# The last w2 product one accumulator at a time, and the gate product directly behind it

## The chip, the cores and the metric

The kernel runs on one core of a Trainium2 chip. The metric is device time in microseconds (us). Each time is one execution; the median of the runs is what counts.

## The reference

```python
def _attn_ref(q, k, v, tau):                   # batch 4, heads 8, seq 576, head_dim 64
    scores = scale * np.matmul(q, k.transpose(0, 1, 3, 2))
    thresh = np.max(scores, axis=-1, keepdims=True) - tau
    scores = np.where(scores >= thresh, scores, -1000000000.0)
    ...
    return np.matmul(attn, v)                  # softmax over the kept scores

def _moe_ref(x, w_gate, w1, w2):               # x [2304, 512], 8 experts, F = 1024
    cap = N // E                               # 288 tokens for every expert
    order = np.argsort(-(x @ w_gate).flatten())
    ...                                        # greedy: best free token/expert pair first
    for e in range(E):
        h = np.maximum(x[mask] @ w1[e], 0.0)
        out[mask] = h @ w2[e]

def _moe2_ref(x, w_gate, w_val, w_out):        # d_ff = 1536
    gate = 1.0 / (1.0 + np.exp(-(x @ w_gate)))
    return gate * (x @ w_val) @ w_out

def reference(...):
    x = attn_out.transpose(0, 2, 1, 3).reshape(B * S, H * D)
    x = _moe_ref(x=x, **moe_kwargs)
    return _moe2_ref(x=x, **moe2_kwargs)
```

## The kernel before

Attention fills the first 365 us or so, in an order written out in a hand table; the change does not touch it. After it the function `experts` does the rest expert by expert, with x, h and y held transposed (features on the partitions, the 288 tokens of one expert along the free axis).

Each float32 operand of a product is held as two parts, a rounded high half and the remainder, and a product of two such operands is three products: high·high, low·high, high·low. With 128-wide slices each product of the program is therefore a run of 12 matmuls of 128x128 by 128x288. High halves are written by ACT, low halves by DVE: `yh`, `xh`, `hh`, `gh` are ACT's, `yl`, `xl`, `hl`, `gl` are DVE's. The first expert's w1 and w2 products are the exception, they are plain float32.

For expert e:

- `arrive(e)`: POOL gathers the rows of x (`xr`, `xs`); PE turns them with twelve transposes in four triples (`ps<-idf,xr` twice and `ps<-idf,xs` once, L1191), and each triple is evicted by `xh` (ACT) and `xl` (DVE, L1142).
- `stage_m(e)`: eight times a w1 product (`ps<-xh,w`, L1147, in a work buffer of PSUM, evicted with relu by `hh` and `hl`) and a w2 product (`acc<-hh,w` and `acc<-hl,w`, L1157, onto four accumulators). Weights `wr` come on SP's queue (L1219, three buffers) and are split by ACT (`w<-wr`, L1228) and DVE (L1055). The four accumulators are then evicted into y: four `yh` on ACT (L1136) and four `yl` on DVE (L1142).
- `stage_g(e)`: twelve times a gate product G (`ps<-yh,wgh` ..., eight matmuls with `yh`, then four with `yl`), a value product V (`ps<-yh,wvh` ...), the sigmoid `sg` (ACT, L1329), `gt` (DVE, L1333), `gh` (ACT, L1337), `gl` (DVE, L1340), and an out product (`acc<-gh,wo`). The weights of G and V stay in SBUF; those of the out product, `wo`, are loaded on SP (L1311). At the end the four accumulators are evicted into `ot`, turned back by 12 transposes (`rows`, `ps<-idf,ot`, L1378) in three groups of four, evicted (`orow`, L1385) and scattered by POOL (L1389).

The **seam** of an expert, in this text, is the place on PE between its last w2 product and its first value product.

PSUM has four accumulator buffers (`ps_acc`), three work buffers (`ps_work`, shared by the w1, G and V products, the triples and the row transposes), and one for the router. `onto` already writes the last of the eight w2 products accumulator by accumulator, so that the first accumulator is complete after three of the twelve matmuls.

Beside this runs the router, which finds the tokens of the next expert. Its wide rounds search a threshold in 8 steps each: a table `kx<-kc` is stored (L747) and read back as 16 broadcasts `kw<-kx` (L751), both on SP's queue; in each step DVE scans it twice (`big<-kw,tw`, L766), writes `rhw` (L769), and PE adds it up (`rps<-rhw`, L772). There are four wide rounds, 32 steps.

The order of the instructions on each engine is written by a planner, `Plan`, before anything runs. Each job has an engine, a planned duration, jobs it depends on, a priority, and buffers it takes or holds. `step` places, over and over, the job that can start first on its engine by the planner's clock. PE has a main chain, the products in their order (`m_seq` and `g_seq`; `main` gives its next job); its other jobs (triples, row transposes, router steps) go first if they are ready by the time PE comes free, and otherwise fill the time until the main chain's head is ready. The last w2 product is one job in this plan: all four `yh` jobs depend on all of it, and G(0) depends on the first three `yh`.

```python
a = job("PE", 1.59, g1, (ydep if j else yhi[:3]) + [ready[3 * j]], None, acq=[hpg], use=hy[e])
a.order = ydep
```

Of the kernel before, what the change touches and what calls it, by code (L numbers as in the profile page):

```python
# [904 lines left out]
class Job:  # L905


    def __init__(self, eng, dur, fn, deps, prio, acq, use, lag):
        self.eng, self.dur, self.fn, self.deps, self.prio, self.acq, self.use, self.lag = eng, dur, fn, deps, prio, acq, use, lag
        self.end, self.order, self.quick = None, [], False  # L910


class Slots:
# [11 lines left out]
class Plan:  # L925
# [16 lines left out]
    def job(self, eng, dur, fn, deps=(), prio=0.0, acq=(), use=(), lag=0.0):  # L942
        j = Job(eng, dur, fn, [d for d in deps if d is not None], prio, acq, use, lag)
        for h in (*acq, *use):
            h.left += 1
        if prio is not None:
            self.queue(j, prio)
        return j
# [24 lines left out]
        return t  # L973

    def step(self):
        best = None
        for e, todo in self.todo.items():
            cand = todo if e == "PE" else todo[:120]
            can = [(r, j) for j in cand for r in [self.ready(j)] if r is not None]
            if e == "PE":  # L980
                main = [(r, j) for j in self.main() for r in [self.ready(j)] if r is not None]
                late = [(r, j) for r, j in can if (r + j.lag if j.prio != -1 else max(r + j.lag, self.spaced)) <= self.free[e]]
                can = late + main + [x for x in can if x not in late]
            free, crit = self.free[e], self.crit
            if crit is not None and crit.eng == e and crit.end is None:
                c = self.ready(crit)
                if c is not None:
                    can = [(r, j) for r, j in can if j is crit or max(r, free) + j.dur <= c]
            if not can:
                continue  # L990
            t = max(free, min(r for r, _ in can))
            if best is None or t < best[0]:
                best = t, next(j for r, j in can if r <= t)
        if best is None:
            return False
        t, j = best
        if j in self.todo[j.eng]:
            self.todo[j.eng].remove(j)
        self.place(t, j)
        return True  # L1000
# [26 lines left out]
def experts(tc, rt, xd, idf, w12, w3in, w3, pre, out):  # L1027
    nc = tc.nc
    V, A, G, SP = nc.vector, nc.scalar, nc.gpsimd, nc.sync
    with (  # L1030
# [14 lines left out]
        job = p.job  # L1045
        big, wdcap, pw, acc = Slots(9), Slots(WD), Slots(3), Slots(1)
# [12 lines left out]
        ready, stored, first_out, first_hold = {}, {}, {}, {}  # L1059
        for n in range(36):  # L1060
            j, kind = divmod(n, 3)
# [85 lines left out]
                nc.tensor.matmul(ps, w(q), x[:, q], start=n == 0, stop=n == 11)  # L1147
                n += 1

        def onto(acc, wh, wl, xh, xl, first, last):  # L1150

            parts = [(i, m) for i in range(3) for m in range(4)]
            if last:
                parts.sort(key=lambda q: q[::-1])
            for i, m in parts:
                w, x = ((wh, xh), (wl, xh), (wh, xl))[i]
                nc.tensor.matmul(acc[m][:, :CAP], w[:, 128 * m : 128 * m + 128], x, start=first and i == 0, stop=last and i == 2)  # L1157
# [47 lines left out]
        def stage_m(e):  # L1205

            seq1, seq2 = [], []
            x_dep = xl_jobs[e]
            hacc = Hold(acc)
            accs = {}  # L1210
            ws = []
            for j in range(8):
                base = pos_m[e] + 2 * j
                hr, h0, h1, hps, hh = Hold(s_wr), Hold(s_w0), Hold(s_w1), Hold(pw), Hold(s_h)
                box = {}

                def load(e=e, j=j, box=box):
                    box["r"] = wp.tile([128, 2, 512], F32, name="wr", bufs=3)
                    SP.dma_start(box["r"], w12[bass.ds(reg[e], 1), j].rearrange("a p (h f) -> (a p) h f", h=2))  # L1219
                    return 524288  # L1220

                ld = job("SP", 0.4, load, [expert_job[e]], base - 10, acq=[hr])
                half = [ld, ld]
                for i, (nm, hd) in enumerate((("w0", h0), ("w1", h1))):

                    def hi(i=i, nm=nm, box=box):
                        box[nm] = wp.tile([128, 2, 512], F32R, name=nm)
                        A.activation(box[nm][:, 0], box["r"][:, i], AF.Copy)  # L1228

                    def lo(i=i, nm=nm, box=box):  # L1230
                        minus(box[nm][:, 1], box["r"][:, i], box[nm][:, 0])

                    pr = base + 2.5 * i - 3
                    if e:
                        a = job("ACT", 0.56, hi, [ld], pr, acq=[hd], use=[hr])
                        half[i] = job("DVE", 0.64, lo, [a], pr, use=[hd, hr])

                def m1(e=e, box=box):
                    box["ps"] = ps_w.tile([128, 512], F32, name="ps")
                    if e == 0:  # L1240
                        for q in range(4):
                            nc.tensor.matmul(
                                box["ps"][:, :CAP], box["r"][:, 0, 128 * q : 128 * q + 128], X[0][0][:, q], start=q == 0, stop=q == 3
                            )
                        return
                    w = box["w0"]
                    thrice(
                        box["ps"][:, :CAP], lambda q: w[:, 0, 128 * q : 128 * q + 128], lambda q: w[:, 1, 128 * q : 128 * q + 128],
                        *X[e],
                    )  # L1250

                def evh(box=box):
                    dt = F32R if e else F32
                    box["h"] = hp.tile([128, CAP], dt, name="hh", bufs=3), hp.tile([128, CAP], dt, name="hl", bufs=3)
                    two(*box["h"], box["ps"][:, :CAP], relu=True)

                def evl(box=box):
                    two_l(*box["h"], box["ps"][:, :CAP], relu=True)

                def m2(j=j, box=box):  # L1260
                    if j == 0:
                        accs["a"] = [ps_a.tile([128, 512], F32, name="acc") for m in range(4)]
                    if e == 0:
                        for m in range(4):
                            nc.tensor.matmul(
                                accs["a"][m][:, :CAP], box["r"][:, 1, 128 * m : 128 * m + 128], box["h"][0], start=j == 0, stop=j == 7
                            )
                        return
                    onto(accs["a"], box["w1"][:, 0], box["w1"][:, 1], *box["h"], j == 0, j == 7)

                own = [h0] if e else [hr]
                a = job("PE", 1.59 if e else 2.12, m1, [half[0]] + x_dep, None, acq=[hps], use=own + hx[e])
                b = job("ACT", 0.32, evh, [a], base - NEAR, acq=[hh], use=[hps])
                if e:
                    b = job("DVE", 0.39, evl, [b], base - NEAR, use=[hps, hh])
                own = [h1] if e else [hr]
                c = job("PE", 1.59 if e else 2.12, m2, [b, half[1]], None, acq=[hacc] if j == 0 else [], use=own + [hh] + ([hacc] if j else []))
                seq1.append(a)
                seq2.append(c)
            ydep, yhi = [], []  # L1280
            for m in range(4):

                def evh(m=m):
                    if m == 0:
                        Y[e] = [bt(h, [128, 4, CAP], f"y{x}", F32R) for h, x in zip(hy[e], "hl")]
                    two(Y[e][0][:, m], Y[e][1][:, m], accs["a"][m][:, :CAP])

                def evl(m=m):
                    two_l(Y[e][0][:, m], Y[e][1][:, m], accs["a"][m][:, :CAP])

                pr = pos_m[e] + 16 - NEAR
                a = job("ACT", 0.32, evh, [c], pr, acq=hy[e] if m == 0 else [], use=[hacc] + (hy[e] if m else []))
                a.order = yhi[:1]
                yhi.append(a)
                ydep.append(job("DVE", 0.39, evl, [a], pr, use=[hacc] + hy[e]))
            m_seq[e] = seq1[:2] + [x for j in range(2, 8) for x in (seq2[j - 2], seq1[j])] + seq2[6:]
            stage_g(e, ydep, yhi)

        def stage_g(e, ydep, yhi):
# [4 lines left out]
            for j in range(12):  # L1304
# [40 lines left out]
                    w = box["wo"] if e else first_out[j]  # L1345
                    onto(accs["a"], w[:, 0], w[:, 1], *box["h"], j == 0, j == 11)

                a = job("PE", 1.59, g1, (ydep if j else yhi[:3]) + [ready[3 * j]], None, acq=[hpg], use=hy[e])
                a.order = ydep
                s = job("ACT", 0.31, sig, [a], base - NEAR, acq=[hsg], use=[hpg])  # L1350
                b = job("PE", 1.59, lambda g1=g1: g1(nm="v"), ydep + [ready[3 * j + 1]], None, acq=[hpv], use=hy[e])
                g1s.append([a, b])
# [206 lines left out]
```

## Time and profile before

| | us |
|---|---|
| median of 3 runs | 1126.08 (1125.22 to 1126.72) |
| the profiled execution | 1126.27 |
| span in its trace | 1124.5 |
| PE, PEld busy | 1053.8, 980.8 |
| DVE, ACT, POOL busy | 788.4, 524.1, 322.5 |

PE is TensorE's matmuls, PEld its weight loads, DVE VectorE, ACT ScalarE, POOL GpSimd, and SPq the DMA queue that SP feeds. All times below are of one profiled execution, in us from the start of the span, which ends 1.8 us short of that execution's own time. The mean granted TensorE clock is 0.983 of full speed.

### The profile page before, as it was taken

Reading aid. Unit: us, or ns where it says so; the run is one execution under the profiler, and the core shown is the slowest. Engines: PE = TensorE matmul, PEld = TensorE weight load, DVE = VectorE, ACT = ScalarE, POOL = GpSimd, SP = SyncE. Lnnn points to the kernel's source line nnn. Section 1 sums busy time; section 2 is a strip of 40 time slices with the busy share of each in tenths; the row PEclk is TensorE's granted clock in tenths of the full one; section 3 lists DMA queues with packets and bytes.
Section 4 is the critical chain, followed back from the end, with each engine's and each line's share of the span. In section 5 each row is a group of like instructions: output and inputs, shape, how many; then the busy total and the mean of one; then the engine's idle time right before and its main releaser. Section 6 shows DMA issues by size and latency. Waiting matters only on the chain.

```text
span 1124.5 us, 21000 instructions
## 1 busy us (share of the span) xinstructions
PE 1053.8 (94%) x7885; PEld 980.8 (87%) x7885; DVE 788.4 (70%) x1915; ACT 524.1 (47%) x1176; POOL 322.5 (29%) x334
## 2 busy tenths in 40 slices
PE   3999999999994899998998999999999999999997
PEld 3788888888883579998997999999999899999996
DVE  7899999999988999876876867866864313412311
ACT  4788898889882233343133125214313413412411
POOL 5888988898840100020010011010101100100101
PEclk9999999999996899999999999999999999999999
DMA  7422424334015676546356347346444433433232
GB/s 265 166 87 98 145 87 137 107 133 139 1 39 201 215 276 241 183 155 161 110 145 186 94 121 211 113 119 179 146 117 152 134 112 119 162 107 123 76 108 84
DMA packets 52885, 156.17 MB, mean 139 GB/s; under 512 B 11568, under 2 KB 16560, under 8 KB 50864
## 3 DMA queue, kind: packets, MB, share of 16 engines
q1 hardware_dynamic: 49712, 145.40, 40.6%
q0 software_dynamic: 3072, 9.44, 2.8%
q8 instruction: 62, 1.02, 0.4%
q14 instruction: 39, 0.32, 0.1%
HBM read 135.38 MB, written 19.43 MB: 138 GB/s over the span
## 4 chain that ended last, share of the span: by engine, by line
PE 53%; issue 26%; DVE 13%; DMA 4%; POOL 2%; ACT 1%; SPq 1%; DVEq 0%; POOLq 0%; ACTq 0%
PE ps L1147 19%; PE acc L1157 11%; PE s L250 7%; PE t L291 4%; PE o L367 2%; PE o L391 2%; DVE nm L261 2%; PE o L375 2%; PE o L363 2%; DVE p L283 1%; DMA wr<-in_w 1%; POOL out L1389 1%; DMA qkr<-in_qk 1%; DVE lo L348 1%; DVE wf L1091 1%
## 5 line engine op out<-in xcount | busy, mean ns | idle before, releaser
L1333 DVE TENSOR_TENSOR gt<-ps,sg 128x288 f32<-128x288 f32 x96 | 43.8, 457 | 146.1 <-PE ps L1147 132.2
L1389 POOL DMA_INDIRECT out<-orow,idx x24 | 22.9, 952 | 423.3 <-ACT orow L1385 397.2
L1329 ACT ACTIVATE sg<-ps 128x288 f32<-128x288 f32 x96 | 39.5, 412 | 199.0 <-PE ps L1147 173.3
L1157 PE MATMUL acc<-gh,wo 128*128 128x288 f32 x768 | 123.0, 298 | 0.0
L265 ACT ACTIVATE e<-s,nm 128x576 f32<-128x576 f32 x144 | 106.3, 738 | 24.8 <-DVE nm L261 23.4
L1055 DVE TENSOR_TENSOR w<-wr,w 128x512 fp32r<-128x512 f32 x112 | 75.4, 689 | 60.1 <-ACT w L1228 59.6
L1147 PE MATMUL ps<-yh,wgh 128*128 128x288 f32 x384 | 107.2, 301 | 9.6 <-DVE xl L1142 7.2
L1337 ACT ACTIVATE gh<-gt 128x288 fp32r<-128x288 f32 x96 | 42.7, 445 | 155.7 <-DVE gt L1333 154.0
L283 DVE SCALAR_TENSOR_TENSOR p<-s,th,e 128x576 f32<-128x576 f32 x128 | 100.7, 810 | 16.2 <-ACT th L269 14.0
L1157 PEld LDWEIGHTS acc<-gh,wo 128*128 128x128 f32 x768 | 108.0, 188 | 1.7 <-issue 1.4
L261 DVE TENSOR_REDUCE nm<-s 128x1 f32<-128x576 f32 x144 | 104.2, 748 | 6.5 <-PE s L250 5.5
L1147 PE MATMUL ps<-yh,wvh 128*128 128x288 f32 x384 | 106.2, 299 | 0.0
L1147 PE MATMUL ps<-yh,wgl 128*128 128x288 f32 x384 | 105.6, 297 | 0.0
L1228 ACT ACTIVATE w<-wr 128x512 fp32r<-128x512 f32 x112 | 69.0, 629 | 77.9 <-PE acc L1157 32.5
L1147 PE MATMUL ps<-yh,wvl 128*128 128x288 f32 x384 | 104.9, 296 | 0.0
L1172 POOL DMA_INDIRECT xr<-xd,idx x16 | 15.2, 950 | 308.1 <-issue 208.8
L250 PE MATMUL s<-kh,qs 128*128 128x288 f32 x320 | 80.1, 333 | 24.2 <-DVE p L283 15.8
L250 PEld LDWEIGHTS s<-kh,qs 128*128 128x128 f32 x320 | 52.9, 197 | 41.9 <-issue 22.8
L1147 PEld LDWEIGHTS ps<-yh,wgh 128*128 128x128 f32 x384 | 72.7, 189 | 10.9 <-DVE xl L1142 5.7
L766 DVE TENSOR_SCALAR_CACHE_REDUCE big<-kw,tw 128x1152 bf16<-128x1152 f32 x56 | 79.0, 1410 | 1.2
L291 PE MATMUL t<-idf,p 128*128 128x128 f32 x548 | 78.2, 276 | 0.7 <-ACT lo L346 0.7
L291 PEld LDWEIGHTS t<-idf,p 128*128 128x128 f32 x548 | 64.5, 142 | 11.7 <-ACT tf L321 2.6
(233 smaller groups left out, 2766.3 us busy)
## 6 DMA issues: line engine op xcount, KB each, us to landing
wo<-wod SPq DMA_DIRECT2D x84, 512.0 KB, 3.6
wr<-in_w SPq DMA_DIRECT2D x64, 512.0 KB, 3.8
qkr<-in_qk SPq DMA_DIRECT2D x15, 1248.0 KB, 5.4
wd<-in_w SPq DMA_DIRECT2D x36, 512.0 KB, 4.4
wod<-wo SPq DMA_DIRECT2D x12, 512.0 KB, 3.4
vr<-in_v SPq DMA_DIRECT2D x16, 320.0 KB, 3.8
kw<-kx SPq DMA_DIRECT2D x64, 72.0 KB, 4.4
xd<-xl SPq DMA_DIRECT2D x8, 512.0 KB, 6.5
```

Source lines behind the costliest of these rows:

```text
L250: nc.tensor.matmul(s[:, h, 0:288], qs[:, qo : qo + 128], kt[:, ko + 288 * h : ko + 288 * h + 288], start=m == 0, stop=m == len(src) - 1,)
L261: nc.vector.tensor_reduce(d[u]["nm", i], d[u]["s", i][:, :, 0:288], op=OP.max, axis=AX.XY, negate=True)
L265: nc.scalar.activation(e, d[u]["s", i][:, :, 0:288], AF.Exp, bias=d[u]["nm", i])
L283: nc.vector.scalar_tensor_tensor(dst.rearrange("p (c n) -> p c n", c=2), w["s", i][:, :, 0:288], nmth[n // 2][1][:, n % 2 : n % 2 + 1], w[ ...
L291: nc.tensor.matmul(t[:m, 128 * j : 128 * j + 128], src, idf, is_transpose=True, start=j == 0, stop=j == len(srcs) - 1, skip_group_check=True,)
L766: v.tensor_scalar(self.big, self.kw[h], thr, None, op0=OP.is_ge, op1=OP.add, accum_out=cnt[:, h : h + 1])
L1055: V.tensor_sub(l, x, h.bitcast(F32))
L1147: nc.tensor.matmul(ps, w(q), x[:, q], start=n == 0, stop=n == 11)
L1157: nc.tensor.matmul(acc[m][:, :CAP], w[:, 128 * m : 128 * m + 128], x, start=first and i == 0, stop=last and i == 2)
L1228: A.activation(box[nm][:, 0], box["r"][:, i], AF.Copy)
L1333: V.tensor_tensor(box["gt"], box["v"][:, :CAP], box["sg"], op=OP.mult)
L1337: A.activation(box["h"][0], box["gt"], AF.Copy)
```

## The change

The last w2 product (j = 7) becomes four jobs of the plan, one for each accumulator, three matmuls each; `yh` of accumulator m depends on the m-th of them alone. G(0) depends on the first `yh` only. And PE is reserved: G(0) carries a mark, `seam`, that names the first `yh`. As soon as that `yh` has its place in the plan and G(0) is the next job of the main chain but not ready, `step` passes PE over as long as any other engine has something to place, so that nothing is put on PE between the w2 product and G(0).

```diff
     def step(self):
+        return self.choose(True) or self.choose(False)
+
+    def choose(self, keep):
...
             if e == "PE":
-                main = [(r, j) for j in self.main() for r in [self.ready(j)] if r is not None]
+                heads = self.main()
+                main = [(r, j) for j in heads for r in [self.ready(j)] if r is not None]
+                if keep and heads and heads[0].seam and heads[0].seam.end is not None and not (main and main[0][1] is heads[0]):
+                    continue
...
-                c = job("PE", 1.59 if e else 2.12, m2, [b, half[1]], None, acq=[hacc] if j == 0 else [], use=own + [hh] + ([hacc] if j else []))
-                seq1.append(a)
+                own = own + [hh] + ([hacc] if j else [])
+                dur = 1.59 if e else 2.12
+                if j < 7:
+                    c = [job("PE", dur, m2, [b, half[1]], None, acq=[hacc] if j == 0 else [], use=own)]
+                else:
+                    c = [job("PE", dur / 4, lambda m=m, m2=m2: m2(ms=[m]), [b, half[1]], None, use=own) for m in range(4)]
+                seq1.append([a])
                 seq2.append(c)
...
-                a = job("ACT", 0.32, evh, [c], pr, acq=hy[e] if m == 0 else [], use=[hacc] + (hy[e] if m else []))
+                a = job("ACT", 0.32, evh, [c[m]], pr, acq=hy[e] if m == 0 else [], use=[hacc] + (hy[e] if m else []))
...
-                a = job("PE", 1.59, g1, (ydep if j else yhi[:3]) + [ready[3 * j]], None, acq=[hpg], use=hy[e])
-                a.order = ydep
+                a = job("PE", 1.59, g1, (ydep if j else yhi[:1]) + [ready[3 * j]], None, acq=[hpg], use=hy[e])
+                a.order, a.seam = ydep, yhi[0]
```

The instructions are the same and as many; each engine runs them in another order from the first seam on (the lines move by 7 to 13). Three places show it.

PE at the second expert's seam, from the end of its last w2 product; `w_7235` is that product's weight tile, L1191 (after: L1198) are the transposes of the next expert's rows. Before:

```order
L1157 MATMUL acc<-hh,w_7235 128x288 x2
L1157 MATMUL acc<-hl,w_7235 128x288
L1191 MATMUL ps<-idf,xr 128x96 x2
L1191 MATMUL ps<-idf,xs 128x96
L1191 MATMUL ps<-idf,xr 128x96 x2
L1191 MATMUL ps<-idf,xs 128x96
L1191 MATMUL ps<-idf,xr 128x96 x2
L1191 MATMUL ps<-idf,xs 128x96
L1147 MATMUL ps<-yh,wgh 128x288
L1147 MATMUL ps<-yh,wgl 128x288
```

After:

```order
L1164 MATMUL acc<-hh,w_7235 128x288 x2
L1164 MATMUL acc<-hl,w_7235 128x288
L1154 MATMUL ps<-yh,wgh 128x288
L1154 MATMUL ps<-yh,wgl 128x288
L1154 MATMUL ps<-yh,wgh 128x288
L1154 MATMUL ps<-yh,wgl 128x288
L1154 MATMUL ps<-yh,wgh 128x288
L1154 MATMUL ps<-yh,wgl 128x288
L1154 MATMUL ps<-yh,wgh 128x288
L1154 MATMUL ps<-yh,wgl 128x288
L1154 MATMUL ps<-yl,wgh 128x288 x4
L1198 MATMUL ps<-idf,xr 128x96 x2
```

The gate product now follows the w2 product at once. One triple went ahead of the w2 product, two follow the gate product.

ACT at the same place. Before:

```order
L1228 ACTIVATE w_7274<-wr 128x512
L1136 ACTIVATE xh<-ps 128x288
L1228 ACTIVATE w_7290<-wr 128x512
L1228 ACTIVATE w_7303<-wr 128x512
L1136 ACTIVATE yh<-acc 128x288 x4
L1136 ACTIVATE xh<-ps 128x288 x3
L1329 ACTIVATE sg<-ps 128x288
```

After:

```order
L1235 ACTIVATE w_7274<-wr 128x512
L1143 ACTIVATE xh<-ps 128x288
L1143 ACTIVATE yh<-acc 128x288 x3
L1235 ACTIVATE w_7302<-wr 128x512
L1143 ACTIVATE yh<-acc 128x288
L1235 ACTIVATE w_7309<-wr 128x512
L1342 ACTIVATE sg<-ps 128x288
L1143 ACTIVATE xh<-ps 128x288 x2
```

Two weight conversions stood ahead of the four `yh`; now three `yh` stand ahead of both, and one of the conversions is between the third and the fourth.

SP's queue in the third expert's w1 and w2 products: `wr` are their weights, `kx` and `kw` the router's table. Before:

```order
L1311 DMA wo<-wod_5001 128x1024
L747 DMA kx<-kc 128x8x18
L1219 ISA
L1219 DMA wr<-in_w 128x1024
L751 DMA kw<-kx 16x1152
L1219 ISA
L1219 DMA wr<-in_w 128x1024
L751 DMA kw<-kx 16x1152 x7
L1219 ISA
L1219 DMA wr<-in_w 128x1024
```

After:

```order
L1324 DMA wo<-wod_5001 128x1024
L1226 ISA
L1226 DMA wr<-in_w 128x1024
L747 DMA kx<-kc 128x8x18
L1226 ISA
L1226 DMA wr<-in_w 128x1024
L751 DMA kw<-kx 16x1152 x4
L1226 ISA
L1226 DMA wr<-in_w 128x1024
L751 DMA kw<-kx 16x1152 x6
```

One weight load moved ahead of `kx`, and the table's reads fall into other groups between the loads.

## Rows read from the trace of the kernel before

**Rows 1.** Page, part 1: busy time, share of the span, instructions.

```profile
PE 1053.8 (94%) x7885; PEld 980.8 (87%) x7885; DVE 788.4 (70%) x1915; ACT 524.1 (47%) x1176; POOL 322.5 (29%) x334
```

**Rows 2.** Page, part 5: busy, mean ns | idle before, releaser.

```profile
L1147 PE MATMUL ps<-yh,wgh 128*128 128x288 f32 x384 | 107.2, 301 | 9.6 <-DVE xl L1142 7.2
```

**Rows 3.** Stretches, PE alone: bounds, length, busy (count), clock, DMA share, GB/s.

```profile
419.32:422.98 3.66, 3.15 (x14) 1.00 0.69 243
514.42:519.56 5.14, 2.61 (x23) 1.00 0.96 245
610.44:615.85 5.41, 2.61 (x24) 1.00 0.63 218
702.21:706.31 4.10, 3.17 (x18) 1.00 0.38 113
790.70:795.24 4.54, 3.02 (x26) 1.00 0.54 174
880.10:888.32 8.22, 5.79 (x39) 0.83 0.65 199
970.00:974.74 4.74, 3.64 (x30) 1.00 0.70 232
1055.84:1058.82 2.98, 2.98 (x26) 1.00 0.00 0
598.32:610.44 12.12, 9.71 (x67) 1.00 0.66 186
```

**Rows 4.** Timeline, second expert's seam: start, length, engine, line, instruction, count [idle before].

```profile
515.16 1.29 ACT L1136 ACTIVATE yh<-acc 128x288 fp32r<-128x288 f32 x4
515.89 1.55 DVE L1142 TENSOR_TENSOR yl<-acc,yh 128x288 fp32r<-128x288 f32 x4
517.35 1.18 DVE L1142 TENSOR_TENSOR xl<-ps,xh 128x288 fp32r<-128x288 f32 x3
517.86 0.40 PE L1147 MATMUL ps<-yh,wgh 128*128 128x288 f32 x1 [2.53 <-DVE xl L1142]
```

**Rows 5.** Timeline, last expert's seam.

```profile
1054.82 1.64 ACT L1136 ACTIVATE yh<-acc 128x288 fp32r<-128x288 f32 x4 [1.58 <-PE acc L1157]
1055.26 1.68 DVE L1142 TENSOR_TENSOR yl<-acc,yh 128x288 fp32r<-128x288 f32 x4 [1.53 <-ACT yh L1136]
1055.84 1.47 PE L1378 MATMUL ps<-idf,ot 128*96 128x128 f32 x12
1057.13 0.40 PE L1147 MATMUL ps<-yh,wgh 128*128 128x288 f32 x1
1058.82 0.30 PE L1147 MATMUL ps<-yh,wvh 128*128 128x288 f32 x1
```

**Rows 6.** Timeline, PE: a triple within an out product; the sixth expert's G.

```profile
673.86 0.33 PE L1191 MATMUL ps<-idf,xr 96*128 96x96 f32 x2
674.05 0.52 PE L1157 MATMUL acc<-gh,wo 128*128 128x288 f32 x2
...
885.42 0.46 PE L1147 MATMUL ps<-yh,wgh 128*128 128x288 f32 x1 [1.87 <-DVE xl L1142]
```

**Rows 7.** Timeline, third expert's w1 and w2 products: SP's queue, ACT.

```profile
585.63 0.37 SPq L747 DMA_DIRECT2D kx<-kc  x1
591.31 0.35 SPq L1219 DMA_DIRECT2D wr<-in_w  x1
597.31 1.15 ACT L1228 ACTIVATE w<-wr 128x512 fp32r<-128x512 f32 x2 [3.15 <-DMA wr<-in_w]
```

**Rows 8.** Timeline, a wide round of the router: PE's wait, DVE's scan and slack.

```profile
530.57 0.17 PE L772 MATMUL rps<-rhw,one 128*128 128x8 bf16 x1 [1.31 <-DVE rhw L769]
545.58 0.46 DVE L1333 TENSOR_TENSOR gt<-ps,sg 128x288 f32<-128x288 f32 x1 [0.48 <-PE rps L772]
546.53 1.41 DVE L766 TENSOR_SCALAR_CACHE_REDUCE big<-kw,tw 128x1152 bf16<-128x1152 f32 x1
550.47 0.46 DVE L1333 TENSOR_TENSOR gt<-ps,sg 128x288 f32<-128x288 f32 x1 [0.49 <-PE rps L772]
```

More of the change, by code (lines that the diff above doesn't have):

```diff
@@ L909, in __init__ @@
         self.eng, self.dur, self.fn, self.deps, self.prio, self.acq, self.use, self.lag = eng, dur, fn, deps, prio, acq, use, lag
-        self.end, self.order, self.quick = None, [], False
+        self.end, self.order, self.quick, self.seam = None, [], False, None
 class Slots:
@@ L1148, in thrice, with onto @@
                 n += 1
-        def onto(acc, wh, wl, xh, xl, first, last):
-            parts = [(i, m) for i in range(3) for m in range(4)]
+        def onto(acc, wh, wl, xh, xl, first, last, ms=range(4)):
+            parts = [(i, m) for i in range(3) for m in ms]
             if last:
@@ L1258, in evl, with m2 @@
                     two_l(*box["h"], box["ps"][:, :CAP], relu=True)
-                def m2(j=j, box=box):
+                def m2(j=j, box=box, ms=range(4)):
                     if j == 0:
@@ L1263, in m2 @@
                     if e == 0:
-                        for m in range(4):
+                        for m in ms:
                             nc.tensor.matmul(
@@ L1268, in m2 @@
                         return
-                    onto(accs["a"], box["w1"][:, 0], box["w1"][:, 1], *box["h"], j == 0, j == 7)
+                    onto(accs["a"], box["w1"][:, 0], box["w1"][:, 1], *box["h"], j == 0, j == 7, ms)
                 own = [h0] if e else [hr]
@@ L1295, in stage_m @@
                 ydep.append(job("DVE", 0.39, evl, [a], pr, use=[hacc] + hy[e]))
-            m_seq[e] = seq1[:2] + [x for j in range(2, 8) for x in (seq2[j - 2], seq1[j])] + seq2[6:]
+            seq = seq1[:2] + [x for j in range(2, 8) for x in (seq2[j - 2], seq1[j])] + seq2[6:]
+            m_seq[e] = [x for y in seq for x in y]
             stage_g(e, ydep, yhi)
```

## The prediction

> **What bounds the kernel now.** I read the busy shares first: PE is at 94% of the span and its weight loads at 87%, against 70% for DVE, 47% for ACT and 29% for POOL [rows 1]. So time can only be won where PE stands still or runs slowly. Next come the groups by line: of the products of the expert stages, the one with real idle time ahead of it is the gate product, 9.6 us, of which 7.2 us ended with DVE's `xl`, an eviction of transposed rows of the next expert [rows 2]. These waits lie at the seams, and the eight seams as stretches (the first eight of rows 3: from the end of the last w2 product to the first value matmul) are 3.66, 5.14, 5.41, 4.10, 4.54, 8.22, 4.74 and 2.98 us [rows 3].
>
> What such a stretch needs is read at the last expert, where the row transposes cover everything: twelve of them start at 1055.84, G starts at 1057.13 and V at 1058.82 [rows 5]. The transposes thus need 1057.13 − 1055.84 = 1.29 and G 1058.82 − 1057.13 = 1.69. Four row transposes are a third, 0.43. A triple of the arriving rows starts at 673.86 and the next product at 674.05, 0.19 [rows 6]; I take 0.25, since that product's first pair is long.
>
> Why the others take more shows best at the second expert [rows 4]. Three triples fill all three work buffers of PSUM. ACT has two weight conversions ahead of the `yh` in its order and begins the first `yh` at 515.16, 0.74 after the w2 product (514.42, the stretch's start). DVE follows with four `yl` until 517.44 and only then does the `xl` that frees a buffer; G starts at 517.86 after 2.53 idle. It is a queueing loss, not a lack of engine time.
>
> **Part 1, the seams: what is lost before.** Stretch minus need (G, plus what is turned inside it):
> - experts 0 to 2: 3.66 − 1.69 − 0.25 = 1.7 (a small product of the router stands there, taken like a triple); 5.14 − 1.69 − 0.75 = 2.7; 5.41 − 1.69 − 0.75 = 3.0;
> - experts 3 and 4: 4.10 − 1.69 − 0.25 = 2.2; 4.54 − 1.69 − 0.86 − 0.25 = 1.7;
> - expert 5: 8.22 − 1.69 − 1.29 − 1.0 = 4.2 (12 row transposes and all four triples). Here the granted clock is 0.83 against 1.00 at the other seams [rows 3]: G starts at 885.42 after 1.87 idle [rows 6] and takes 888.32 − 885.42 = 2.90, so 1.2 of the loss is G partly at the lower level of the clock, 1.2 GHz, behind an idle PE;
> - experts 6 and 7: 4.74 − 1.69 − 1.29 − 0.25 = 1.5; 2.98 − 1.29 − 1.69 = 0.
>
> Sum 17.0 us. The transposes themselves are moved, not removed, and cost the same wherever they stand.
>
> **Part 2, the seams: what is left after.** With G directly behind the w2 product, G(0) waits for `yh` and `yl` alone. The last expert bounds this from below: its first `yh` began at 1054.82, 1.02 before the product's end, the four `yh` ended at 1056.46 and the four `yl` at 1056.94 [rows 5]. A G at 1055.84 would reach its fourth `yh` pair after six matmuls (0.13 each, 1.69/12 rounded down) at 1056.63 and its fourth `yl` matmul at about 1057.3, both later than needed: no wait. The bound from above is that every `yh` still begins 0.74 after the product, as at the second expert. Then the four `yl` end 517.44 − 514.42 = 3.02 behind the product, the last matmul of G follows, and the stretch is about 3.3 instead of 1.69: 1.6 lost at each seam. Where each lies between is set by ACT's and DVE's new order:
> - expert 0: two conversions (1.15 / 2 = 0.6 each [rows 7]) still precede `yh`: 0.7. Expert 1: one conversion between the third and fourth `yh`, and V waits a little for the sigmoid's buffer: 0.7;
> - expert 2: all work buffers are taken by triples ahead of the product, G's is freed by an `xl` behind three `yl`: 1.2. Expert 3: a conversion and an `xh` ahead of the first `yh`, a conversion within: 1.2;
> - expert 4: a router scan of 1.41 [rows 8] stands ahead of `yl` on DVE, partly under the product: 0.9. Experts 5 to 7: 0.4, 0.1, 0.1, with `yh` first in line; at expert 5 PE no longer stands idle, so the clock should hold at 1.00.
>
> Sum 5.3, between 0 and 8 × 1.6 = 13. Seams: 17.0 − 5.3 = **11.7 gained**, between 4 and 17.
>
> **Part 3, what the new order moves elsewhere.**
> - *SP's queue at expert 2.* `kx` is issued at 585.63, and the weight load behind its first read only at 591.31; ACT later waits 3.15 for `wr` [rows 7]. PE's stretch 598.32 to 610.44 is 12.12 with 9.71 busy [rows 3]. It holds five products of 1.6 and some small work of 0.4, so 12.12 − 8.4 = 3.7 are lost. After, one weight load stands ahead of `kx` and the next right behind it. Bounds: 0 and 3.7; I take 2.4, because two of the three late loads move forward.
> - *The router.* At the second expert PE waits 1.31 for `rhw` [rows 8]; how much of that wait stays when everything around it moves is not in the rows; I take 0.8 gained, between a wait twice as long (−1.3) and none (1.3), nearer to none, since in SP's order three more of the table's reads now stand ahead of the weight load of that round, and the wait is for scans of that table.
> - *New costs.* At the last expert three triples now stand directly ahead of the first w1 product, which needs their `xh` and `xl`: the eviction of one, about 0.65 (half of the 1.29 for four `yh`). At the sixth, triples within a value/out pair, 0.25. At the third, a second `rhw` wait, 0.4. Together 1.3 lost, between 0 and 3.
>
> Sum of part 3: 2.4 + 0.8 − 1.3 = **1.9 gained**, between −4 and 5.
>
> **The sum.** 11.7 + 1.9 = 13.6 against the profiled execution's 1126.27: 1112.7. That execution lies 0.2 above the median of the runs, 1126.08, so on the median's footing 1112.5.
>
> **The rivals.**
>
> *Exposed eviction at every seam.* The transposes were the work that covered the eviction of the accumulators; with nothing between, a G that needs `yh` and `yl` waits for them. By the upper bound of part 2 this leaves 1.1 to 1.6 a seam, say 9 to 10 of the 17, and gives about 1126 − 8 = 1118. Against it stands the last expert, where eviction begins under the product itself [rows 5]; for it the second, where it did not [rows 4]. The Trainium skill, page Perfetto Trace Analysis, section Optimizing Tensor Performance, says under Matmuls that independent matmul groups should rotate through PSUM banks so that the evacuation of one overlaps the next group's matmuls; that speaks against this change, which takes the independent group out. The last expert's rows agree only in part: their eviction overlaps the same product's later matmuls as well.
>
> *Absorbed downstream.* PE arrives sooner at waits that other engines pace: `rhw` [rows 8], weight loads [rows 7]. If half of what experts 1 to 4 gain at their seams (9.6 − 4.0 = 5.6) and all of the 1.9 goes there: 1112.5 + 2.8 + 1.9 = 1117; with expert 2's starvation made worse by 2, 1119. For it: these waits exist. Against: after them PE runs back to back, so a gain at a later seam cannot be taken away by an earlier wait.
>
> *Slower.* In a wide round's steps DVE's order had `gt` ahead of the first of the two scans; now it stands between them, and PE's router product between G and V. A step has DVE waiting 0.48 and 0.49 for `rps`, with a period of 550.47 − 545.58 = 4.89 [rows 8], about one G, V and out product. If the second scan slips by more than that slack, each step lengthens. At 0.6 a step beyond the slack, in 30 of the 32 steps, 18 us are lost: 1112.5 + 18 = 1130.5. It turns slower from 13.6 / 30 = 0.45 a step. Against it: `gt` waits only for V, which PE now ends sooner relative to the scan, and 0.48 of slack stands ready.
>
> *It doesn't do what it says.* The order still shows four row transposes ahead of G at expert 6 and the router's product at expert 2; were PE stalled at all seams by something else named in no row, the time stays near 1126.
>
> **How the numbers follow.** Forecast 0.74, exposed eviction 0.11, absorbed 0.09, slower 0.04, no change 0.02 for the last. The predicted time is the forecast's, 1112.5. Its own spread is the unknown residue at the seams (5.3, from 0 upward) and part 3: down by 5.5 to 1107, if nearly no residue stays; up to the two rivals' 1118 and 1119, so the range ends at 1120. What lies outside is the slower case, no change, and tails of the forecast. A measurement here tells about 0.2% (2.3 us) from no change; faster by more than that, below 1123.8, is everything but the last two rivals and a tail: 0.93, same 0.03, slower 0.04.
>
> **What would show it.** In the profile after: the eight stretches between 1.7 and 3.0, with no `xl` as the releaser of `ps<-yh,wgh`; at each seam the first `yh` beginning before the last w2 matmul; the clock at 1.00 at the sixth seam; shorter waits for `wr` around 600; a wide round's step at 4.9 or less. The forecast is wrong if G's waits merely change their name to `yl`, or if the idle time before `rps<-rhw` grows by more than a few us.

## The result, and the profile after

The changed kernel takes 1114.11 us (1113.41 to 1114.60, four runs) against 1126.05 for the kernel before on the same chip: ratio 0.989, 95% interval 0.988 to 0.991. That is 12 us gained, where 13.6 were forecast, and within the range given. The profiled execution took 1113.79 us.

Page, part 1 of the changed kernel, beside [rows 1], and the gate product's line, beside [rows 2]:

```profile
PE 1051.8 (95%) x7884; PEld 979.3 (88%) x7885; DVE 787.2 (71%) x1915; ACT 525.1 (47%) x1176; POOL 323.5 (29%) x334
...
L1154 PE MATMUL ps<-yh,wgh 128*128 128x288 f32 x384 | 106.0, 298 | 2.1 <-DVE xl L1149 1.2
```

Busy times hardly move; the idle time ahead of the gate product falls from 9.6 to 2.1 us. The eight seams, from the end of the last w2 product to the first value matmul, answer to the first eight of [rows 3] (bounds, length, PE busy and count, clock, DMA share, GB/s):

```profile
419.01:421.27 2.26, 2.26 (x15) 1.00 0.49 150
512.87:515.52 2.65, 2.51 (x20) 1.00 0.79 252
604.50:607.58 3.08, 1.84 (x15) 1.00 0.03 8
694.56:697.76 3.20, 2.56 (x17) 1.00 0.13 53
783.64:787.44 3.80, 3.63 (x23) 1.00 0.74 226
873.19:876.29 3.10, 3.09 (x22) 1.00 0.50 168
957.90:960.29 2.39, 2.39 (x23) 1.00 0.59 159
1044.28:1045.88 1.60, 1.60 (x14) 1.00 0.00 0
```

The sum falls from 38.8 to 22.1, and the clock is 1.00 in all of them, also at the sixth, which showed 0.83 before. Not all of the 16.7 is gained, since some transposes now stand elsewhere. The last stretch is G alone: 1.60. With that as the work of G (the prediction took 1.69), 0.11 for a row transpose, 0.25 for a triple and 0.2 for a router product (the prediction took 0.25), what a stretch holds beyond its work is its loss; the eight sum to 17.3 us before and 5.5 after. At the second expert the change looks like this (timeline, beside [rows 4]):

```profile
512.03 1.05 ACT L1143 ACTIVATE yh<-acc 128x288 fp32r<-128x288 f32 x3
512.48 1.18 DVE L1149 TENSOR_TENSOR yl<-acc,yh 128x288 fp32r<-128x288 f32 x3
512.87 0.30 PE L1154 MATMUL ps<-yh,wgh 128*128 128x288 f32 x1
512.98 0.62 ACT L1235 ACTIVATE w<-wr 128x512 fp32r<-128x512 f32 x1
513.50 0.40 ACT L1143 ACTIVATE yh<-acc 128x288 fp32r<-128x288 f32 x1
```

The first `yh` begins 0.84 us before the product ends at 512.87; before, it began 0.74 after it. The conversion between the third and the fourth `yh` still costs G 0.4.

### The profile page after: what moved, and what is told of

Same layout as the page of the kernel before. It is cut to its first block, busy times and chain, and to the rows that moved or that the text cites. A ratio compares the mean times of both kernels' runs of the same rounds, so it can differ in the third digit from the quotient of the medians.

```text
span 1112.0 us, 20994 instructions
## 1 busy us (share of the span) xinstructions
PE 1051.8 (95%) x7884; PEld 979.3 (88%) x7885; DVE 787.2 (71%) x1915; ACT 525.1 (47%) x1176; POOL 323.5 (29%) x334
## 3 DMA queue, kind: packets, MB, share of 16 engines
q8 instruction: 62, 1.02, 0.4%
## 4 chain that ended last, share of the span: by engine, by line
PE 53%; issue 26%; DVE 11%; DMA 4%; ACT 2%; POOL 2%; SPq 1%; POOLq 0%; DVEq 0%; ACTq 0%
PE ps L1154 18%; PE acc L1164 10%; PE s L250 7%; PE t L291 4%; PE o L367 2%; PE o L391 2%; DVE nm L261 2%; PE o L375 2%; DMA wr<-in_w 2%; PE o L363 2%; DVE p L283 1%; PE acc L1272 1%; POOL out L1402 1%; DVE big L766 1%; DVE lo L348 1%
## 5 line engine op out<-in xcount | busy, mean ns | idle before, releaser
L291 PEld LDWEIGHTS t<-idf,p 128*128 128x128 f32 x548 | 64.8, 143 | 11.7 <-ACT tf L321 2.5
```

The costliest lines, as they stand in the source:

```text
L291: nc.tensor.matmul(t[:m, 128 * j : 128 * j + 128], src, idf, is_transpose=True, start=j == 0, stop=j == len(srcs) - 1, skip_group_check=True,)
```

## The experiments

Each ratio is to the kernel before, on the same chip. The first four experiments share one chip, the next four a second and the last two a third, so between these groups ratios are compared and not times. Two theories stood against each other. The prediction's: turned rows between w2 product and gate product fill the work buffers of PSUM, and G waits for their `xl`. The rival: what counts is when `yh` and `yl` come, whatever PE does between.

**Without the reservation of PE.**

```diff
-                if keep and heads and heads[0].seam and heads[0].seam.end is not None and not (main and main[0][1] is heads[0]):
-                    continue
```

> The changed kernel without the reservation of PE: the last w2 product is still four planned jobs and G(0) depends on the first yh, but PE may take other work. By the planned order the turned rows stand between the last w2 product and G again (experts 1 to 7: 9, 6, 3, 3 transposes of arriving rows, 4 row transposes and 6, 12 and 4 row transposes). Theory (the seams lose because turned rows fill the three work buffers and their evictions share ACT and DVE with yh and yl): experts 1, 2 and 5 lose 2 to 3 us again with xl as the releaser of the gate product, the seams together 11 to 13 us instead of 5.5, time 1120 to 1122 us. Rival (the early start of yh alone brings the gain): seams near 6 us, time 1114 to 1116 us.

Measured: 1115.09 us, ratio 0.991 (0.989 to 0.993). My theory missed. The transposes are back, but the seams lose 5.2 us, no more than in the changed kernel. The second expert shows why: the same nine transposes stand there as before, yet G idles 0.61 instead of 2.53 (timeline, beside [rows 4]):

```profile
512.74 1.49 ACT L1141 ACTIVATE yh<-acc 128x288 fp32r<-128x288 f32 x4
513.16 1.55 DVE L1147 TENSOR_TENSOR yl<-acc,yh 128x288 fp32r<-128x288 f32 x4
...
513.61 0.33 PE L1196 MATMUL ps<-idf,xr 96*128 96x96 f32 x2
...
514.12 1.01 ACT L1141 ACTIVATE xh<-ps 128x288 fp32r<-128x288 f32 x3
...
514.63 1.18 DVE L1147 TENSOR_TENSOR xl<-ps,xh 128x288 fp32r<-128x288 f32 x3
514.99 1.18 ACT L1233 ACTIVATE w<-wr 128x512 fp32r<-128x512 f32 x2
515.13 0.40 PE L1152 MATMUL ps<-yh,wgh 128*128 128x288 f32 x1 [0.61 <-DVE xl L1147]
```

The product ends at 513.61. `yh` and `yl` ran under it, `xl` followed at once, and the two weight conversions came last. In the kernel before, one of these conversions stood ahead of `yh` and itself waited for the last w2 product, as its own row shows:

```profile
514.62 0.63 ACT L1228 ACTIVATE w<-wr 128x512 fp32r<-128x512 f32 x1 [0.42 <-PE acc L1157]
```

`yh` stands behind that conversion in ACT's order, so it could not begin under the product. The same holds at the third, fifth, sixth and seventh expert: each time the last conversion ahead of `yh` begins only 0.2 us after the w2 product's end (timeline; the products of the first three of these end at 610.44, 790.70 and 880.10):

```profile
610.69 0.63 ACT L1228 ACTIVATE w<-wr 128x512 fp32r<-128x512 f32 x1 [1.39 <-PE acc L1157]
...
790.90 0.63 ACT L1228 ACTIVATE w<-wr 128x512 fp32r<-128x512 f32 x1 [0.35 <-PE acc L1157]
...
880.30 0.63 ACT L1228 ACTIVATE w<-wr 128x512 fp32r<-128x512 f32 x1 [0.97 <-PE acc L1157]
```

**With the reservation, without the quarters.** PE is held empty from the whole product to G (more strictly than in the change, which lets a job through once G's start is known). That G(0) depends on the first `yh` only is part of this run and of the first one alike.

```diff
-                if j < 7:
-                    c = [job("PE", dur, m2, ...)]
-                else:
-                    c = [job("PE", dur / 4, ...) for m in range(4)]
+                c = [job("PE", dur, m2, ...)]
...
-                a = job("ACT", 0.32, evh, [c[m]], pr, ...)
+                a = job("ACT", 0.32, evh, c, pr, ...)
```

> The opposite half: PE is kept free between the last w2 product and G (nothing between at any of the eight seams), but that product is one planned job again and all yh depend on the whole of it. Theory (a bare seam costs the eviction of the accumulators, unless it begins under the product): the first yh begins about 0.3 us behind the product, the last yl ends 2.2 to 2.6 behind it, each seam loses 1.3 to 1.6 us, together 10.5 to 12.5 instead of 5.5, time 1119 to 1121 us. Rival (only the transposes had to go, the quarters do not matter): seams near 5.5, time 1114 to 1115 us.

Measured: 1124.13 us, ratio 0.999 (0.998 to 1.001): no difference that can be told. The seams lose 12.6 us, the upper end of what the theory expected; the time is worse than it expected, since the 4.7 gained at the seams brought only 3.3 in the profile (1122.96). The stretches and the line of the gate product:

```profile
514.08:518.06 3.98, 2.96 (x21) 1.00 0.79 250
609.33:613.44 4.11, 3.04 (x18) 1.00 0.77 250
699.48:703.34 3.86, 2.84 (x18) 1.00 0.45 154
...
L1154 PE MATMUL ps<-yh,wgh 128*128 128x288 f32 x384 | 107.3, 302 | 6.3 <-ACT yh L1143 6.2
```

No `xl` releases G any more, but `yh` does, for 6.2 us: the wait has changed its name. So seven of the eight bare seams cost 1.3 to 2.3 us. The last expert's costs nothing: nothing stands ahead of `yh` on ACT there, and the first `yh` begins at 1050.95, 1.02 before the product ends, as it did in the kernel before [rows 5]. The accumulators were always finished one by one on the chip; what the quarters change is where the plan puts `yh` in ACT's order. The two halves of the change, each alone, are thus worth at most some 3 us (reservation: 1.6 by the medians, 3.3 in the profile, no difference that can be told) and 11 (quarters).

**`yh` and `yl` first.** From the first quarter of the last w2 product, ACT and DVE too take nothing else that would not end before the next `yh` or `yl` can start.

```diff
+            if keep and e in ("ACT", "DVE"):
+                for c0, ys in self.ys:
+                    pend = [j for j in ys if j.eng == e and j.end is None]
+                    if c0.end is not None and pend:
+                        lim = min((r for j in pend for r in [self.ready(j)] if r is not None), default=c0.end + 0.1)
+                        can = [(r, j) for r, j in can if j in pend or max(r, free) + j.dur <= lim]
```

> The changed kernel, and from the first quarter of the last w2 product on ACT and DVE too are kept for yh and yl: weight conversions, xh, xl and router scans that would not end before the next yh or yl can start are planned behind them. Nothing stands between w2 product, gate product and value product at any seam. Theory (what is left at the seams, 5.5 us, is queueing behind that other work: 1.3 us each at experts 2, 3 and 4): the seams lose 0 to 2 us together, a gain of 3.5 to 5 us there; what is pushed behind costs up to 2 us elsewhere; time 1109.5 to 1112.5 us. Rival (the eviction itself is exposed): each seam still loses about 0.7, time 1113 to 1115 us.

Measured: 1113.11 us, ratio 0.989 (0.987 to 0.991), the same as the change. At the seams it is exactly what was expected: seven are of the form w2 product, G, V (at one expert the plan runs the next expert's w1 and w2 products first), and six of them last 1.58 to 1.62. The first lasts 1.82, since G begins at 419.69 there, ahead of the bound of the first row here.

```profile
419.80:421.51 1.71, 1.71 (x15) 1.00 1.02 374
513.05:514.64 1.59, 1.59 (x14) 1.00 0.57 203
599.71:601.29 1.58, 1.58 (x14) 1.00 0.89 208
```

At these seams the eviction itself is not exposed. But the profiled execution (1112.28) is 14.0 faster than before's where the seams gained 17.1: 3.1 are lost elsewhere. Rows of the timeline show where, in the fourth expert's products:

```profile
659.79 1.33 PE L1161 MATMUL ps<-xh,w 128*128 128x288 f32 x8 [0.51 <-DVE xl L1156]
666.78 1.54 PE L1171 MATMUL acc<-hh,w 128*128 128x288 f32 x7 [0.73 <-ACT ot L1388]
...
717.94 0.17 PE L772 MATMUL rps<-rhw,one 128*128 128x8 bf16 x1 [0.73 <-DVE rhw L769]
718.90 0.40 PE L1171 MATMUL acc<-hh,w 128*128 128x288 f32 x1 [0.56 <-DVE w L1069]
```

PE waits for a turned row's `xl`, for `ot`, for the router and for late weights.

**No transposes from the last w1 product on.**

```diff
+                if keep and heads and heads[0].tail:
+                    can, late = [x for x in can if not x[1].acq], [x for x in late if not x[1].acq]
```

> The changed kernel, and transposes are also kept off PE from the last w1 product to G(0), so that no triple takes a work buffer that the last hh/hl or G(0) needs. Theory: at the third expert the 1.3 us that PE idles ahead of six transposes and the 1.2 us that G waits for xl go; the rest of the seams stays as it is; 1.5 to 2.5 us gained, time 1111.5 to 1112.7 us. Rival (the wait moves to the eviction of the triples elsewhere): within 0.7 us of the changed kernel, 1113.4 to 1114.8 us.

Measured: 1114.05 us, ratio 0.990 (0.987 to 0.992): the rival holds, no gain over the change. At the third expert the wait of G for `xl` is gone, but its last w2 product now waits 1.60 for an `hl`, which stands behind a weight conversion and a router scan on DVE.

**SP's queue planned with its measured costs.**

```diff
-                yield "SP", 0.45, "kw2" if h or e else "kw"
+                yield "SP", 0.6, "kw2" if h or e else "kw"
...
-            j.end = self.dma + 2.5
+            j.end = self.dma + (4.5 if more == 73729 else 2.5)
```

(73729 marks the store of the table.) It ran beside the changed kernel, unaltered:

> The changed kernel unaltered, as the yardstick for the three beside it on this chip: 1113 to 1115 us, and the ratio to the kernel before 0.988 to 0.991.

> The changed kernel; the planner is told what SP's queue really costs in a wide round: 0.60 us for one read of the router's table (it assumed 0.45; 14 of them took 8.33) and 4.5 us from issue to landing for the table's store (it assumed 2.5; the read behind it began 3.2 to 5.2 later). Weight loads so get their place between the reads. Theory (what the seams gave back is partly lost again because weight loads of the third and fourth expert wait behind those reads; losses outside the seams there sum to about 3 us in the changed kernel): the waits on wr and on w conversions near 600 and 690 us fall below 1 us together, 1.5 to 3 us gained, 1111 to 1112.7 us. Rival (the transfers themselves, not their order, set the pace; or later reads delay the router's scans by as much): within 0.7 us of the changed kernel.

Measured: 1112.44 us, ratio 0.989 (0.986 to 0.991), for the changed kernel, and 1112.71, 0.988 (0.986 to 0.991), with the loads timed: no gain. No wait on weights or their conversions is left near 600 and 690 us, but row transposes at 665 us wait 2.17 us for an `xl`. The yardstick is of use by itself: its profiled execution took 1111.46, 2.3 less than the other one of the same kernel, above. Of that, 1.3 lies at the fourth expert, where weight conversions had waited up to 1.46 for `wr` and the first `yh` had come late; this time no product waited for weights there.

> Both: ACT and DVE kept for yh and yl at the seams, and SP's queue planned with the measured costs. Theory (two separate losses, 5.5 us at the seams and about 5 us of late weights in the kernel that only kept ACT and DVE free): seams at 0 to 0.5 us together, losses outside them 3 to 4 us smaller than there, 1108.5 to 1110.5 us. Rival (the seams' gain is always given back at the next wait): 1112 to 1114 us.

Measured: 1109.68 us, ratio 0.985 (0.983 to 0.987). The two edits that brought nothing alone bring 2.8 us together, as the theory wanted: all five runs lie below all five of the changed kernel beside it, though the two intervals overlap a little. The seams lose 0.7 us, a little more than the 0.5 expected.

**Four times the gate multiplication**, to price the rival that was to make the change slower.

```diff
-                    V.tensor_tensor(box["gt"], box["v"][:, :CAP], box["sg"], op=OP.mult)
+                    for _ in range(4 if 1 <= e <= 4 else 1):
+                        V.tensor_tensor(box["gt"], box["v"][:, :CAP], box["sg"], op=OP.mult)
```

> The changed kernel, but DVE does the multiplication gt four times over (same operands, same result) in experts 1 to 4, where the wide rounds run; the order of all engines is that of the changed kernel but for these repeats. It prices the rival that was to make the change slower. In a wide round's step DVE waits 0.5 us; three more gt take 3 x 0.37 = 1.1 us. Theory (beyond its slack a step grows one for one): 0.6 us a step in some 30 steps, 16 to 20 us slower than the changed kernel, 1129 to 1135 us, a step of 5.5 us instead of 4.90. Rival (the step is paced by the tensor engine's three products with room to spare, and DVE's repeats hide): under 5 us slower.

Measured: 1148.83 us, ratio 1.021 (1.017 to 1.024), 36 us slower than the changed kernel beside it. A step of a wide round, on DVE:

```profile
545.48 0.16 DVE L775 TENSOR_REDUCE n<-rps 128x1 int32<-128x8 f32 x1
...
547.41 1.93 DVE L1347 TENSOR_TENSOR gt<-ps,sg 128x288 f32<-128x288 f32 x4
...
551.27 0.16 DVE L775 TENSOR_REDUCE n<-rps 128x1 int32<-128x8 f32 x1
```

The step is 551.27 − 545.48 = 5.79 instead of 4.90, with no wait for `rps` left. The scan that follows begins 1.85 after the first of the four `gt`, and 0.37 after a single one, so the three added cost 1.48, not 1.1; less the slack of 0.5 that is 0.98, near the 0.89 measured. In 30 steps 0.89 makes 27 us; the rest was not traced to a cause, but it lies in the same four experts, which between their seams took 35 us longer than in the changed kernel beside it. So the rival's mechanism is real and its slack of half a microsecond is all there is, but the change left it alone, as two rows of the changed kernel show (period 544.24 − 539.34 = 4.90, wait 0.51 and 0.50, beside [rows 8]):

```profile
539.34 0.17 DVE L775 TENSOR_REDUCE n<-rps 128x1 int32<-128x8 f32 x1 [0.51 <-PE rps L772]
...
544.24 0.17 DVE L775 TENSOR_REDUCE n<-rps 128x1 int32<-128x8 f32 x1 [0.50 <-PE rps L772]
```

**`yh` and `yl` first, PE not reserved.** The edit of the third experiment without the two lines that the first took out; then the same with the loads timed.

> ACT and DVE kept for yh and yl at the seams as in the third experiment, but PE not reserved: turned rows stand between the last w2 product and G where the plan puts them (experts 1 to 7: 6, 0, 3, 8, 8, 4 and 8 transposes, and a router product at the third). Revised theory (what costs at a seam is when yh and yl come on ACT and DVE, and transposes on PE in between are cover, not cause): the seams lose at most 2 us together beyond their work, as little as with the reservation within 1.5 us; time 1110 to 1114 us. Rival, the theory of the prediction (transposes between fill the work buffers and G waits for their xl): 2 us and more lost at three or more seams, time above 1115 us.

Measured: 1113.28 us, ratio 0.988 (0.985 to 0.990). The time is what the revised theory expected, the seams are not: they lose 5.0 us, nothing at four experts (3, 5, 6 and 7, counted from 0) although up to eight transposes stand there, but 0.6 at expert 0 and 1.1, 1.9 and 1.4 at 1, 2 and 4, where G waits for a work buffer (releasers `xl` and `orow`):

```profile
L1159 PE MATMUL ps<-yh,wgh 128*128 128x288 f32 x384 | 106.2, 299 | 3.9 <-ACT orow L1404 2.9 <-DVE xl L1154 0.9
```

So full work buffers do cost, 1 to 2 us where they happen. They are the second cause, not the first: 5.0 us in this run, where `yh` is early, against 12.6 where only `yh` is late.

> The same with SP's queue planned by the measured costs, the counterpart without reservation of the seventh experiment (ratio 0.985 there). Revised theory: the reservation of PE is worth nothing, ratio 0.983 to 0.987. Rival (the reservation is worth something once ACT and DVE are out of the way): 2 us slower than that one or more, ratio 0.987 or above.

Measured: 1108.44 us, ratio 0.984 (0.982 to 0.985), the best of all, faster than the changed kernel (0.989) by an interval that does not overlap. The reservation brings nothing in the time here either: at the seams it saves 5 us (5.0 against 0.2) or 2.5 (3.2 against 0.7, with the loads timed), and the kernel loses as much elsewhere. That this happens where the transposes land instead is likely, but was not traced.

| kernel | yh may start early | PE reserved | yh, yl ahead of all | seams lose, us | ratio |
|---|---|---|---|---|---|
| before | no | no | no | 17.3 | 1 |
| whole product, reserved | no | yes | no | 12.6 | 0.999 |
| quarters alone | yes | no | no | 5.2 | 0.991 |
| the change | yes | yes | no | 5.5 | 0.989 |
| y first, reserved | yes | yes | yes | 0.2 (seven seams) | 0.989 |
| y first, free | yes | no | yes | 5.0 | 0.988 |
| y first, reserved, loads timed | yes | yes | yes | 0.7 (seven seams) | 0.985 |
| y first, free, loads timed | yes | no | yes | 3.2 | 0.984 |

## Why the prediction was right, and where not

The number holds by its large terms; one of the reasons behind it does not, and the small term, part 3, came out at less than half in this profile.

*Part 1 and 2, the seams.* The loss before, 17.0 in the prediction, is 17.3 at the prices used here, from the same rows. The loss after was forecast as 5.3 and measured as 5.5, so 11.8 are gained for 11.7. Expert by expert the residues were forecast as 0.7, 0.7, 1.2, 1.2, 0.9, 0.4, 0.1, 0.1 and measured as 0.5, 0.6, 1.3, 1.4, 1.3, 0.6, 0, 0. The queues were read rightly: at expert 3 a conversion and an `xh` precede `yh`, at expert 4 the scan precedes `yl`:

```profile
694.34 0.39 ACT L1143 ACTIVATE xh<-ps 128x288 fp32r<-128x288 f32 x1
...
694.62 1.00 ACT L1143 ACTIVATE yh<-acc 128x288 fp32r<-128x288 f32 x3
...
783.46 1.41 DVE L766 TENSOR_SCALAR_CACHE_REDUCE big<-kw,tw 128x1152 bf16<-128x1152 f32 x1
...
784.80 1.55 DVE L1149 TENSOR_TENSOR yl<-acc,yh 128x288 fp32r<-128x288 f32 x4
```

The upper bound of part 2, 1.6 a seam when `yh` starts behind the product, was too low: the whole product lost 1.3 to 2.3 at seven seams, more than 1.6 at most of them. The sixth seam's clock came back to 1.00 as said.

*The signs.* Four of the eight stretches are longer than the 3.0 named (3.08, 3.10, 3.20, 3.80) and the last is shorter than 1.7. `xl` still releases G at the third expert, for 1.2, which the sign ruled out although part 2 counted on it. The first `yh` begins under the product at seven seams; at expert 3 it begins at 694.62, 0.06 after the end. The clock, the shorter waits for `wr` around 600 (at most 2.7 after 3.7) and the step of 4.90 came as named.

*The reason given for it.* "Three triples fill all three work buffers" was taken from the releaser `xl` [rows 2], and part 2 starts from a G "directly behind the w2 product", as if the empty PE were the cure. That step fails. `xl` was the last in a chain whose delay began at its head: a conversion ahead of `yh` that waited for the w2 product. With `yh` early the same nine transposes cost 0.6 us, and with PE reserved but `yh` late the change is worth nothing that can be measured. The forecast survived because both edits were made together; that is luck, since the reservation alone would have been read from the same rows as the cure.

*Part 3.* Forecast 1.9 gained, measured 0.7 (12.5 in the profiled executions, less 11.8). The two gains are there: in the stretch from the second expert's first V to the third's last w2 product (90.88 long before, 88.98 after, with three triples, 0.75, more in it), 2.7 came back, 0.7 of it the wait for `rhw` (1.31 to 0.60), which leaves 2.0 for SP's queue and whatever else changed there; forecast were 0.8 and 2.4. The term that came out larger is the new costs, 1.3 forecast and 2.0 by difference (2.7 − 0.7). One was priced well, the last expert's first w1 product (0.65 forecast, the last row here). One lies inside the 2.0 of SP's queue and was not foreseen: at 602.56 PE idles 1.30, because a triple there needs a work buffer whose last reader, an `hl`, is still to come.

```profile
534.22 0.17 PE L772 MATMUL rps<-rhw,one 128*128 128x8 bf16 x1 [0.60 <-DVE rhw L769]
...
602.56 0.38 PE L1198 MATMUL ps<-idf,xr 96*128 96x96 f32 x2 [1.30 <-DVE hl L1147]
...
1017.81 1.33 PE L1154 MATMUL ps<-xh,w 128*128 128x288 f32 x8 [0.50 <-DVE xl L1149]
```

Another was missed: four triples in a row ahead of an out product of the fourth expert, with only three work buffers; from 747.48 to 749.14 they take 1.66 instead of 1.0. And the waits for weights at the fourth expert were in this profile and not in the second one, as told above; as two profiles of this kernel lie 2.3 apart, 0.7 against 1.9 is no miss that can be told from noise.

*The rivals.* Exposed eviction had its mechanism right: it is what the whole product shows, 12.6 us. It does not decide the changed kernel, because a product that finishes accumulator by accumulator covers its own eviction where `yh` and `yl` come first: six of the seven seams of that run last 1.58 to 1.62, as long as G alone. The Trainium skill (Perfetto Trace Analysis, Optimizing Tensor Performance) says that independent matmul groups should rotate through PSUM banks so that the evacuation of one overlaps the next group's matmuls. At these seams no run bears that out: with a late `yh` the independent transposes between left a larger loss (17.3) than none (12.6), and with `yh` and `yl` first G needs none. Absorption was wrong for the change (outside the seams 0.7 was gained, not lost), but sets in beyond it: of the 5 us that the third experiment takes out of the seams besides, hardly any reached the time until the loads moved too. The slower rival has its price confirmed, about one for one beyond half a microsecond a step, and was not met.

## What to carry to other kernels

The releaser that a profile names for a wait is the end of a chain: follow it up, through the order of instructions on each engine, to the first one that is late, and ask what that one stood behind. When a group's results must be evicted before the next product can run, finish its accumulators one by one and let the plan know it, so that each eviction depends on its own accumulator and does not fall behind other work on ACT and DVE; here that alone brought 11 of the 12 us. Keeping the tensor engine empty besides brought nothing that could be told. Once such a seam is closed, the next gain needs a second edit at the waits that take over, and either edit alone may show nothing.

## What was not expected of the hardware

One read of the router's table cost up to 0.6 us of SP's queue (14 took 8.33 in the kernel before, 7 took 3.21), and the first read behind the table's store, 74 KB by way of DRAM, began 3.2 to 5.2 us after it, with everything behind that read in the queue waiting. Three more `gt` with the same operands and the same output cost 0.49 each, where `gt` followed by another operation freed DVE after 0.37 and four `yl` in a row, each with an output of its own, took 1.55 together; that the shared output makes the difference was not tested. Two profiled executions of one kernel differed by 2.3 us, 1.3 of it at one expert whose weights came late, so a difference of 2 us in a single profile proves nothing here.
